# Polysketch attention with an MLP behind it: queries' features computed once and repeated through DRAM

## The chip, the cores and the metric

The kernel runs on one core of a Trainium2 chip. The metric is the device time of one execution in microseconds (us). The profile has a span of its own, a little shorter than that time, and all its positions are counted from the span's start. TensorE, VectorE, ScalarE and GpSimd are the four computing engines, each working through its instructions in the order of the program; SyncE issues nearly all transfers.

## What is computed

An attention block with features of degree two in place of the softmax, and an MLP block on its result, all in float32: batch 4, 4 heads, 1088 tokens, 32 values a head, so 128 for a token.

```python
def phi(x):                                   # S1, S2: 8 x 32
    a = np.einsum('rd,bhsd->bhsr', S1, x)     # 8 features
    b = np.einsum('rd,bhsd->bhsr', S2, x)     # 8 more
    return np.einsum('bhsi,bhsj->bhsij', a, b).reshape(*x.shape[:-1], 64)
q_p, k_p = phi(q), phi(k)
kv = np.einsum('bhsf,bhsd->bhfd', k_p, v)
z = np.sum(k_p, axis=2)
num = np.einsum('bhsf,bhfd->bhsd', q_p, kv)
den = np.einsum('bhsf,bhf->bhs', q_p, z)[..., None] + 1e-06
x = num / den                                 # heads side by side: 4 x 1088 x 128
xn = (x - mean(x)) / np.sqrt(var(x) + 1e-06) * g_ln
out = x + np.maximum(xn @ w_ch1, 0.0) @ w_ch2 # 128 -> 512 -> 128
```

The point for this change: a token and head have 16 features, 8 of S1 and 8 of S2, and the 64 values of phi are all products of one of the first with one of the second.

## The kernel before

**Chunks.** The tokens are worked on in nine chunks. Chunks 0 to 7 are halves of the four batch entries (chunk c is half c % 2 of entry c // 2), 512 tokens each, four tiles of 128. Chunk 8 (`LAST`) holds the 64 tokens that are left of each entry, 256 in all, two tiles.

**A chunk's stages.** `query_rows` (L376) turns the queries on VectorE in 32x32 blocks, so that the 128 partitions hold 4 heads x 32 values and the columns the tokens (`qT`). `query_features` (L389) makes the features with the partitions of the result standing for the 64 pairs (i, j), twice over for two halves of the tokens. It doesn't compute 16 features and repeat them: its weights `wa` and `wb` (32 x 64 for a head, L620) hold each row of S1 and of S2 eight times, so TensorE computes each of the 16 features eight times. These are 16 products of 32 rows by 64 columns, each over 256 columns of tokens (128 in chunk 8): for each of `wb` and `wa`, two halves and four heads, into PSUM banks 0 to 3. ScalarE copies the half of `wb` to SBUF (`qb`, L408), and VectorE multiplies it with that of `wa`, still in PSUM, into `qp` (L409), in two instructions each for two heads. `numerators` (L416) multiplies `qp` with the keys' sums `kvz` (L432, banks 0 and 1) and divides by the denominators (L439 to L447) to give `x`. `statistics` (L472 to L486) and `root` (L493 to L503) give mean and variance. `turn_x` (L514), or `send_x` with `blocks_x`, transposes x: from chunk 3 on, `send_x` (L518) writes x to DRAM in four transfers (L527), reads it back rearranged in one (`xb`, L533), and `blocks_x` (L540) turns it in blocks. `hidden` (L550, four times, with the ReLU on ScalarE at L553) and `second` (L563) are the MLP, `result` (L578) scales and adds, and four transfers write the output (L599).

The keys go the same way: `key_features` (L320, in PSUM, copied at L325), `key_products` (L338), `key_values` (L355, copied into `kvz` at L363 and L365). Theirs belong to batch entries 0 to 3, and are done by slot 4.

**Order.** There is no scheduler: each engine executes its instructions in the order in which the code emits them. That order is written out by hand, in a part ahead of the loop (to L733) and a loop over slots c = 2 to 8 (L735). Slot c computes the MLP of chunk c, the numerators of chunk c + 2, and, last, the query features of chunk c + 3 (L763):

```python
        if c < LAST:
            mlp_in(c, ...)          # hidden, 4 times
            root(c)
        numerators(c + 2)
        send_x(c + 2)
        ...
            second(c)
            query_rows(c + 3)
            result(c)
        query_features(c + 3)
```

SyncE too issues its transfers in this order, and waits in it: `xb` for the four writes of `rows`, the output for VectorE. Transfers take turns over eight completion semaphores, so that each can be issued only when the eighth ahead of it has landed.

**Buffers.** `qT`, `qb`, `qp`, `xb` and most other tiles of the pool `work` have two buffers; the DRAM tile `rows` and the output tile `ob` have three, `x` four.

Of the kernel before, what the change touches and what calls it, by code (L numbers as in the profile page):

```python
# [9 lines left out]
F32 = mybir.dt.float32  # L10
U32 = mybir.dt.uint32
AF = mybir.ActivationFunctionType
ALU = mybir.AluOpType
# [16 lines left out]
def kernel(  # L30
# [9 lines left out]
    moe_w_ch2: bass.AP,  # L40
    out: bass.AP,
):

# [17 lines left out]
    nc = tc.nc  # L63
# [24 lines left out]
    def bank(i):  # L88
        return banks[:, 512 * i : 512 * (i + 1)]
# [277 lines left out]
                kvp[F * (1 - i) : F * (2 - i), 0 : 2 * D1],  # L367
            )

    qTs, qps, xs, rs, mvs, xTs, hTs, xbs = {}, {}, {}, {}, {}, {}, {}, {}  # L370

    def query_steps(b):

# [15 lines left out]
    def query_features(c, between=None):  # L389
# [16 lines left out]
        for h in (2, 0):  # L406
# [6 lines left out]
            if h and between:  # L413
                between()

    def numerators(c):  # L416


        if c > LAST:
            return  # L420
        x = xs[c] = work.tile([P, 512], F32, tag="x", name="x", bufs=4)
        qp, n = qps.pop(c), ntiles(c) // 2
        step = 64 if c < LAST else 32
        for i in range(n):
            for h in range(H):
                for half in range(2):
                    rows = slice(F * half, F * half + F)
                    for u in range(0, P, step):
                        kvz = kvzs[CHUNKS[c][0] if c < LAST else u // 32]
                        t, o = 256 * h + P * i + u, W * i + D1 * h  # L430
                        z = D1 * (h // 2) + (0 if h % 2 == half else 2 * D1)
                        nc.tensor.matmul(  # L432
                            bank(half)[u : u + step, o : o + D1], qp[rows, t : t + step],
                            kvz[rows, z : z + D1], start=True, stop=True,
                        )
        den = small.tile([P, 4 * H], F32, tag="den", name="den")
        rden = small.tile([P, 4 * H], F32, tag="rden", name="rden")
        m = n * H
        nc.vector.tensor_scalar(  # L439
            out=_ap(den, 0, P, 0, [[m, 2], [1, m]]),  # L440
            in0=_ap(banks, 0, P, D, [[512, 2], [D1, m]]),
            scalar1=1e-6, scalar2=None, op0=ALU.add,
        )
        nc.vector.reciprocal(rden[:, 0 : 2 * m], den[:, 0 : 2 * m])
        for half in range(2):
            by_i, by_h = x_steps(c)
            nc.vector.tensor_tensor(  # L447
                out=_ap(x, 0, P, by_i * n * half, [[by_i, n], [by_h, H], [1, D]]),
                in0=_ap(banks, 0, P, 512 * half, [[W, n], [D1, H], [1, D]]),
                in1=_ap(rden, 0, P, m * half, [[H, n], [1, H], [0, D]]),  # L450
                op=ALU.mult,
            )
# [9 lines left out]
    def ntiles(c):  # L462
        return 4 if c < LAST else 2
# [54 lines left out]
    def send_x(c):  # L518

        if c > LAST:  # L520
            return
        x, m = xs[c], D * ntiles(c)
        xb = xbs[c] = work.tile([P, 512], F32, tag="xb", name="xb")

        rows = dram.tile([P, 4 * m], F32, tag="rows", name="rows", bufs=3)
        for p0 in range(4):
            nc.sync.dma_start(  # L527
                out=bass.AP(
                    rows.tensor, rows.offset + m * p0, [[4 * m, 32], [32 * 4 * m, H], [1, m]]
                ),  # L530
                in_=_ap(x, 32 * p0, 32, 0, [[m, H], [1, m]]),
            )
        nc.sync.dma_start(out=xb[:, 0 : 4 * m], in_=rows)  # L533
# [131 lines left out]
    w1_terms = w1_parts.terms(halves[1])  # L665
    fill(1)


    def keys(b, at):
        for part in range(3):  # L670
# [3 lines left out]
    def keys_in(b):  # L674
        for part in range(3):
            key_tokens(b, part, nc.gpsimd)
            key_rows(b, part)

    def mlp_in(c, between):

        for j in range(JC):
            if j in between:
                between[j]()
            hidden(c, j)
# [17 lines left out]
    for part in range(3):  # L702
# [8 lines left out]
    result(0)  # L711
    query_features(2)
    keys_in(2)

    mlp_in(1, {
        1: lambda: key_values(1, 7, 0, 4),
        2: lambda: query_features(3),
        3: lambda: key_values(1, 7, 4, NT),
    })
    root(1)  # L720
    numerators(2)
# [3 lines left out]
    query_rows(4)  # L725
    numerators(3)
    send_x(3)
    statistics(3)
    second(1, 2, 4)
    turn_x(2)  # L730
    result(1)
# [3 lines left out]
    for c in range(2, LAST + 1):  # L735

        b = (c + 3) // 2
        odd, some = c % 2 == 1, b < B
        if c == LAST - 1:
            blocks_x(LAST)  # L740
        if c < LAST:
            mlp_in(c, {2: lambda: key_values(b, 7, 5, NT)} if some and not odd else {})
            root(c)
        if c == LAST - 1:
            root(LAST)
        numerators(c + 2)
        send_x(c + 2)
        if some and odd:
            keys(b, (2, 3, 7))
        statistics(c + 2)  # L750
        if c < LAST - 1:
            blocks_x(c + 1)
        if c == LAST - 1:
            second(c, 0, 3)
            result(c, 0, 3)
            mlp_in(LAST, {})
            second(c, 3, 4)
            result(c, 3, 4)
        else:
            second(c)  # L760
            query_rows(c + 3)
            result(c)
        query_features(c + 3)  # L763
        if some and odd:
            key_values(b, 7, 0, 5)
        if b + 1 < B and not odd:
            keys_in(b + 1)
# [30 lines left out]
```

## Time and profile before

| | |
|---|---|
| time, median of 3 runs | 114.37 us (114.34 to 115.2) |
| span of the profiled execution | 112.6 us, 4412 instructions |
| TensorE, weight loads beside it | 103.8 us (92%), 73.3 us (65%) |
| VectorE | 62.1 us (55%) |
| ScalarE | 44.0 us (39%) |
| GpSimd | 41.4 us (37%) |
| transfers | 13.13 MB in 12835 packets, mean 117 GB/s |
| products of the query features: L400, `wb` and `wa` | 144 pieces each, 6.0 and 5.5 us busy |
| copies `qb` (L408), products `qp` (L409) | 18 each, 9.3 and 11.1 us busy |
| numerators (L432) | 576 pieces, 10.1 us busy |
| `hidden` (L550), `second` (L563) | 33.9 and 33.1 us busy |

How to read it: the profile calls TensorE's products PE and its weight loads PEld, VectorE DVE, ScalarE ACT, GpSimd POOL, and SyncE's issuing SPq. L400 is line 400 of the kernel. A float32 product appears as two pieces, so the 16 products of a chunk's query features are 32 pieces. Pieces overlap on the array, so their summed durations say less than the chain of work, which follows the end of the kernel back from each piece to what released it. TensorE's granted clock was 1.0 throughout.

### The profile page before, as it was taken

The page shows a single profiled execution, that of the slowest core. Times are in us where ns is not written, and L with a number is a line of the kernel's source. Part 1 is how long each engine was busy: PE and PEld are TensorE (multiplying, and loading weights), DVE is VectorE, ACT ScalarE, POOL GpSimd, SP SyncE. Part 2 cuts the span into 40 slices and gives each one's busy share as a digit, 9 for nine tenths or more (in the row PEclk, how much of TensorE's full clock was granted, in tenths as well). Part 3 has the DMA queues.
Part 4 walks back from the last instruction along what each step waited for, and adds up shares of the span by engine and source line. Part 5 has one row for each costly group of instructions (what it writes and reads, how often), then busy time and mean ns, then how long its engine had stood idle before and what let it go on. Part 6 is the DMA issues. An engine that isn't in the chain of part 4 may idle for free.

```text
span 112.6 us, 4412 instructions
## 1 busy us (share of the span) xinstructions
PE 103.8 (92%) x1875; PEld 73.3 (65%) x1875; DVE 62.1 (55%) x188; ACT 44.0 (39%) x104; POOL 41.4 (37%) x127
## 2 busy tenths in 40 slices
PE   6748889989999999999999999999999999999970
PEld 2336755489745799656953996579449739849760
DVE  1748974958985276621967746129618716320330
ACT  5126445660567430565036403640560262062500
POOL 4053037224898299501450596024003303205000
PEclk9999999999999999999999999999999999999999
DMA  0997999998992000461235043203340350240022
GB/s 12 271 196 218 325 262 243 291 159 266 275 263 89 9 9 0 99 163 29 51 67 167 6 93 124 71 0 74 66 145 13 87 189 6 47 135 4 0 70 70
DMA packets 12835, 13.13 MB, mean 117 GB/s; under 512 B 3472, under 2 KB 9872, under 8 KB 12816
## 3 DMA queue, kind: packets, MB, share of 16 engines
q1 hardware_dynamic: 12720, 12.79, 43.6%
q8 instruction: 14, 0.23, 0.9%
q10 hardware_dynamic: 96, 0.07, 0.3%
q14 instruction: 5, 0.04, 0.1%
HBM read 9.18 MB, written 3.67 MB: 114 GB/s over the span
## 4 chain that ended last, share of the span: by engine, by line
PE 81%; DMA 4%; DVE 4%; SPq 3%; ACT 2%; POOL 2%; issue 1%; ACTq 0%
PE banks L563 29%; PE banks L550 25%; PE banks L432 8%; PE banks L355 7%; PE banks L400 6%; DMA kn<-in_k_dram 4%; PE banks L320 3%; POOL w_cl L198 2%; SPq L126 2%; PE banks L514 1%; DVE qp L409 1%; PE banks L612 1%; SPq L114 1%; ACT xT L516 1%; DVE w_up L211 1%
## 5 line engine op out<-in xcount | busy, mean ns | idle before, releaser
L550 PE MATMUL banks<-xT,w 128*128 128x512 f32 (+1 forms) x72 | 33.9, 595 | 0.6 <-ACT xT L516 0.5
L563 PE MATMUL banks<-w,hT 128*128 128x128 f32 x272 | 33.1, 278 | 0.0
L563 PEld LDWEIGHTS banks<-w,hT 128*128 128x128 f32 x272 | 31.4, 192 | 1.1 <-DVE xT L540 0.2
L553 ACT ACTIVATE hT<-banks 128x512 f32<-128x512 f32 (+1 forms) x36 | 20.7, 574 | 17.5 <-PE banks L550 17.5
L550 PEld LDWEIGHTS banks<-xT,w 128*128 128x128 f32 x72 | 11.9, 189 | 13.3 <-ACT hT L553 5.8
L408 ACT COPY qb<-banks 128x512 f32<-128x512 f32 (+1 forms) x18 | 9.3, 564 | 22.3 <-PE banks L400 22.3
L338 POOL TENSOR_TENSOR kp<-fs 128x1024 f32<-128x1024 f32 (+2 forms) x11 | 15.4, 1426 | 4.8 <-ACT fs L325 4.6
L578 DVE SCALAR_TENSOR_TENSOR ob<-banks,rstd,x 128x128 f32<-128x128 f32 x34 | 9.8, 343 | 10.5 <-PE banks L563 3.7
L498 POOL TENSOR_TENSOR r<-va,r 128x4 f32<-128x4 f32 (+1 forms) x9 | 1.8, 199 | 36.5 <-DVE r L497 30.9
L409 DVE TENSOR_TENSOR qp<-banks,qb 128x512 f32<-128x512 f32 (+1 forms) x18 | 11.1, 656 | 4.6 <-ACT qb L408 4.6
L432 PEld LDWEIGHTS banks<-kvz,qp 64*64 64x64 f32 (+1 forms) x576 | 9.0, 131 | 6.5 <-ACT hT L553 1.5
L497 DVE RECIPROCAL r<-r 128x4 f32<-128x4 f32 (+1 forms) x9 | 1.5, 176 | 19.1 <-ACT r L493 19.1
L432 PE MATMUL banks<-kvz,qp 64*64 64x33 f32 (+1 forms) x576 | 10.1, 219 | 0.8 <-DVE qp L409 0.3
L355 PEld LDWEIGHTS banks<-v,kp 128*32 128x32 f32 (+3 forms) x504 | 7.0, 113 | 4.0 <-issue 1.5
L355 PE MATMUL banks<-v,kp 128*32 128x33 f32 (+3 forms) x504 | 7.9, 202 | 0.0
L400 PE MATMUL banks<-qT,wb 32*64 32x256 f32 (+1 forms) x144 | 6.0, 387 | 1.7 <-DVE qT L289 1.7
L472 DVE BATCH_NORM_STATS2 st<-x 128x6 f32<-128x128 f32 x34 | 7.3, 278 | 0.0
L447 DVE TENSOR_TENSOR x<-banks,rden 128x256 f32<-128x256 f32 (+1 forms) x18 | 6.5, 404 | 0.3
L289 DVE STREAM_TRANSPOSE qT<-qn 128x512 f32<-128x512 f32 x8 | 5.4, 686 | 1.5 <-DMA qn<-in_q_dram 1.5
L320 PE MATMUL banks<-sk,kT 128*64 128x64 f32 x136 | 5.4, 226 | 0.8 <-DVE kT L302 0.4
L320 PEld LDWEIGHTS banks<-sk,kT 128*64 128x64 f32 x136 | 4.7, 137 | 1.9 <-DVE kT L302 0.8
L400 PE MATMUL banks<-qT,wa 32*64 32x256 f32 (+1 forms) x144 | 5.5, 362 | 0.0
(70 smaller groups left out, 83.4 us busy)
## 6 DMA issues: line engine op xcount, KB each, us to landing
out_dram<-ob SPq DMA_DIRECT2D x33, 64.0 KB, 2.2
vn<-in_v_dram SPq DMA_DIRECT2D x16, 128.0 KB, 6.2
kn<-in_k_dram SPq DMA_DIRECT2D x3, 544.0 KB
qn<-in_q_dram SPq DMA_DIRECT2D x3, 544.0 KB
rows<-x SPq DMA_DIRECT2D x20, 64.0 KB, 1.8
xb<-rows SPq DMA_DIRECT2D x5, 256.0 KB, 2.8
kn<-in_k_dram SPq DMA_DIRECT2D x2, 256.0 KB, 3.2
w_raw<-in_moe_w_ch_dram SPq DMA_DIRECT2D x2, 256.0 KB, 2.9
```

The costliest lines, as they stand in the source:

```text
L320: nc.tensor.matmul(kf[u : u + 64, 64 * i : 64 * i + 64], kT[:, P * i + u : P * i + u + 64], sk, start=True, stop=True,)
L338: eng.tensor_tensor(out=_ap(kp, 0, m, (t0 + i0) * H * F, [[F, n], [R, R], [1, R]]), in0=_ap(kf, 0, m, o, [[R2, n], [1, R], [0, R]]), in1=_ ...
L355: nc.tensor.matmul(kvp[o : o + step, D1 * (h // 2) : D1 * (h // 2 + 1)], kp[0:m, H * F * t + f : H * F * t + f + step], v1[0:m, W * t + D1 ...
L400: nc.tensor.matmul(bank(h)[F * half : F * half + F, o : o + n], w[rows, :], qT[rows, n * half : n * half + n], start=True, stop=True,)
L408: nc.scalar.copy(own, _ap(banks, 0, P, 512 * h, [[512, 2], [1, n]]))
L409: nc.vector.tensor_tensor(out=_ap(p, 0, P, 256 * h, [[256, 2], [1, n]]), in0=_ap(banks, 0, P, 512 * h + 256, [[512, 2], [1, n]]), in1=own, ...
L432: nc.tensor.matmul(bank(half)[u : u + step, o : o + D1], qp[rows, t : t + step], kvz[rows, z : z + D1], start=True, stop=True,)
L472: nc.vector.bn_stats(out=st[:, 6 * i : 6 * i + 6], in_=x_tile(c, i))
L550: nc.tensor.matmul(hp[:, 0:n], w1[:, P * j : P * (j + 1)], xTs[c][:, 0:n], start=True, stop=True)
L553: nc.scalar.activation(hTs[c][:, 512 * j : 512 * j + n], hp[:, 0:n], AF.Relu)
L563: nc.tensor.matmul(second_at(c, i), hT[:, 512 * j + P * i : 512 * j + P * i + P], w2[:, DM * j : DM * (j + 1)], start=(j == 0), stop=(j == ...
L578: nc.vector.scalar_tensor_tensor(out=ob[:, t], in0=second_at(c, i), scalar=rstd[:, i : i + 1], in1=x_tile(c, i), op0=ALU.mult, op1=ALU.add,)
```

## The change

For chunks 5 to 8, TensorE computes each of the 16 features once. A new weight tile `wf` (128 x 40, built by GpSimd before the first slots) holds the 8 rows of S1 and of S2 by turns: columns 0 to 31 begin with S1's, columns 8 to 39 with S2's. `send_features` makes 16 products of 32 rows by 32 columns, over 128 columns of tokens (64 in chunk 8): for four quarters u of the tokens and four heads, into 32 partitions of bank h each. Of the 32 columns 16 are used, the two sets of features in one order for the first two quarters and in the other for the last two. One copy of 128 x 512 (ScalarE; VectorE for chunk 5) moves them to SBUF as `ff`, and four transfers write the 16 used partitions of each quarter to DRAM (`feat`, 2 KB a partition).

`spread_features` reads them back repeated: `qa` in one transfer in which each of 16 rows of 4 KB is repeated eight times in neighbouring partitions, and `qb` in two of 64 partitions, each of which repeats a group of eight rows eight times. `query_products` is then one multiplication of 128 x 1024, both operands in SBUF. Since tokens and heads lie in another order in `qp`, `numerators` reads other columns for these chunks.

The stages stand in other slots. The rows of chunk c + 5 are turned and its features made and sent at the end of slot c, where the features of chunk c + 3 were; chunk 6's are made in the middle of slot 2, ahead of the keys' values, and chunk 5's in the middle of slot 1, where VectorE copies them. The reads for chunk c + 4 follow `send_x` of chunk c + 2 in slot c, on the same queue of SyncE, behind those of x. The products of chunk c + 3 stand at the end of slot c. After slot 5 nothing is added. Chunks 0 to 4 keep the old way.

What it is for: TensorE does a smaller part of the array's work for these four chunks, since the repeating is left to the transfers.

```diff
--- before.py
+++ after.py
@@ -367,7 +368,7 @@
                 kvp[F * (1 - i) : F * (2 - i), 0 : 2 * D1],
             )
 
-    qTs, qps, xs, rs, mvs, xTs, hTs, xbs = {}, {}, {}, {}, {}, {}, {}, {}
+    qTs, frows, fqs, qps, xs, rs, mvs, xTs, hTs, xbs = {}, {}, {}, {}, {}, {}, {}, {}, {}, {}
 
     def query_steps(b):
 
@@ -413,6 +414,63 @@
             if h and between:
                 between()
 
+    def send_features(c, eng):
+
+
+
+
+        if c > LAST:
+            return
+        qT, w = qTs.pop(c), 32 * ntiles(c)
+        for u in range(4):
+            for h in range(H):
+                nc.tensor.matmul(
+                    bank(h)[32 * u : 32 * u + 32, 0:w],
+                    wf[D * h : D * h + D, R * (u < 2) : R * (u < 2) + 32],
+                    qT[D * h : D * h + D, w * u : w * u + w], start=True, stop=True,
+                )
+        ff = work.tile([P, 512], F32, tag="ff", name="ff")
+        o, i = _ap(ff, 0, P, 0, [[w, H], [1, w]]), _ap(banks, 0, P, 0, [[512, H], [1, w]])
+        if eng is nc.scalar:
+            eng.copy(o, i)
+        else:
+            eng.tensor_copy(out=o, in_=i)
+
+        rows = frows[c] = dram.tile([32, 8 * w], F32, tag="feat", name="feat", bufs=3)
+        for u in range(4):
+            nc.sync.dma_start(
+                out=bass.AP(
+                    rows.tensor, rows.offset + 8 * w * R2 * (u // 2) + 4 * w * (u % 2),
+                    [[8 * w, R2], [1, 4 * w]],
+                ),
+                in_=ff[32 * u : 32 * u + R2, 0 : 4 * w],
+            )
+
+    def spread_features(c):
+        if c not in frows:
+            return
+        rows, m = frows.pop(c), 256 * ntiles(c)
+        qa = work.tile([P, H * 256], F32, tag="qa", name="qa")
+        qb = work.tile([P, H * 256], F32, tag="qb", name="qb")
+        for t, r0, pat in (
+            (qa, R, [[m, R2], [0, R]]),
+            (qb[0:F], 0, [[0, R], [m, R]]),
+            (qb[F:P], 3 * R, [[0, R], [m, R]]),
+        ):
+            nc.sync.dma_start(
+                out=t[:, 0:m],
+                in_=bass.AP(rows.tensor, rows.offset + m * r0, pat + [[1, m]]),
+            )
+        fqs[c] = qa, qb
+
+    def query_products(c):
+        if c > LAST:
+            return
+        n = 256 * ntiles(c)
+        (qa, qb), p = fqs.pop(c), work.tile([P, H * 256], F32, tag="qp", name="qp")
+        qps[c] = p
+        nc.vector.tensor_tensor(out=p[:, 0:n], in0=qa[:, 0:n], in1=qb[:, 0:n], op=ALU.mult)
+
     def numerators(c):
 
 
@@ -420,7 +478,7 @@
             return
         x = xs[c] = work.tile([P, 512], F32, tag="x", name="x", bufs=4)
         qp, n = qps.pop(c), ntiles(c) // 2
-        step = 64 if c < LAST else 32
+        step, w = (64, 128) if c < LAST else (32, 64)
         for i in range(n):
             for h in range(H):
                 for half in range(2):
@@ -428,6 +486,8 @@
                     for u in range(0, P, step):
                         kvz = kvzs[CHUNKS[c][0] if c < LAST else u // 32]
                         t, o = 256 * h + P * i + u, W * i + D1 * h
+                        if c > 4:
+                            t = w * (H * ((P * i + u) // w) + h) + u % w
                         z = D1 * (h // 2) + (0 if h % 2 == half else 2 * D1)
                         nc.tensor.matmul(
                             bank(half)[u : u + step, o : o + D1], qp[rows, t : t + step],
@@ -664,6 +724,12 @@
     w2_parts.bound(full, nc.gpsimd)
     w1_terms = w1_parts.terms(halves[1])
     fill(1)
+
+    wf = consts.tile([P, 5 * R], F32, name="wf")
+    for w, o, step, n in ((wa, 0, R, 3), (wb, R, 1, 2)):
+        nc.gpsimd.tensor_copy(
+            out=_ap(wf, 0, P, o, [[R2, n], [1, R]]), in_=_ap(w, 0, P, 0, [[0, n], [step, R]])
+        )
 
 
     def keys(b, at):
@@ -711,11 +777,12 @@
     result(0)
     query_features(2)
     keys_in(2)
+    query_rows(5)
 
     mlp_in(1, {
         1: lambda: key_values(1, 7, 0, 4),
         2: lambda: query_features(3),
-        3: lambda: key_values(1, 7, 4, NT),
+        3: lambda: (key_values(1, 7, 4, NT), send_features(5, nc.vector)),
     })
     root(1)
     numerators(2)
@@ -725,7 +792,9 @@
     query_rows(4)
     numerators(3)
     send_x(3)
+    spread_features(5)
     statistics(3)
+    query_rows(6)
     second(1, 2, 4)
     turn_x(2)
     result(1)
@@ -736,15 +805,23 @@
 
         b = (c + 3) // 2
         odd, some = c % 2 == 1, b < B
+
+        def between():
+            if c == 2:
+                send_features(6, nc.scalar)
+            if some and not odd:
+                key_values(b, 7, 5, NT)
+
         if c == LAST - 1:
             blocks_x(LAST)
         if c < LAST:
-            mlp_in(c, {2: lambda: key_values(b, 7, 5, NT)} if some and not odd else {})
+            mlp_in(c, {2: between})
             root(c)
         if c == LAST - 1:
             root(LAST)
         numerators(c + 2)
         send_x(c + 2)
+        spread_features(c + 4)
         if some and odd:
             keys(b, (2, 3, 7))
         statistics(c + 2)
@@ -758,9 +835,10 @@
             result(c, 3, 4)
         else:
             second(c)
-            query_rows(c + 3)
+            query_rows(c + 5)
             result(c)
-        query_features(c + 3)
+        send_features(c + 5, nc.scalar)
+        query_products(c + 3)
         if some and odd:
             key_values(b, 7, 0, 5)
         if b + 1 < B and not odd:
```

## The prediction

> **What bounds the kernel now.** I read the page's busy shares first, then the chain of work that ended last in order of time, then the timeline of one slot, then the transfers by window. From the page:
>
> ```profile
> PE 103.8 (92%) x1875; PEld 73.3 (65%) x1875; DVE 62.1 (55%) x188; ACT 44.0 (39%) x104; POOL 41.4 (37%) x127
> ...
> PE   6748889989999999999999999999999999999970
> ...
> DMA  0997999998992000461235043203340350240022
> GB/s 12 271 196 218 325 262 243 291 159 266 275 263 89 9 9 0 99 163 29 51 67 167 6 93 124 71 0 74 66 145 13 87 189 6 47 135 4 0 70 70
> ```
>
> TensorE is busy in every slice from the ninth on (a slice is 2.8 us). The transfers are full for the first third, and mostly at 0 to 5 tenths after it. A busy share can hide waits, so the chain decides (start us, us, what):
>
> ```profile
> 45.37 1.05 PE banks L400 x32
> ...
> 51.99 1.07 PE banks L432 x64
> 53.06 3.77 PE banks L563 x32
> 56.83 1.05 PE banks L400 x32
> 57.88 3.79 PE banks L550 x8
> 61.66 1.07 PE banks L432 x64
> ...
> 67.69 1.05 PE banks L400 x32
> ...
> 79.05 1.05 PE banks L400 x32
> 80.10 3.79 PE banks L550 x8
> 83.89 1.07 PE banks L432 x64
> ...
> 88.72 0.62 PE banks L400 x32
> ...
> 93.13 0.69 PE banks L432 x47
> ```
>
> From 23 to 102 us the chain is TensorE alone, one piece ending where the next begins. So each microsecond taken off TensorE there comes off the end, until something else is late. The L400 pieces at 56.83, 67.69, 79.05 and 88.72 are the query features of chunks 5, 6, 7 and 8: 3 x 1.05 + 0.62 = 3.77 us. (The one at 45.37 is chunk 4, which stays as it is.)
>
> How late may the new work be? Slot 4 in the timeline:
>
> ```profile
> 79.14 1.12 DVE L578 SCALAR_TENSOR_TENSOR ob<-banks,rstd,x 128x128 f32<-128x128 f32 x4 [0.56 <-POOL va L486]
> 79.88 0.34 SPq L533 DMA_DIRECT2D xb<-rows  x1
> 80.21 1.07 ACT L408 COPY qb<-banks 128x512 f32<-128x512 f32 x2 [5.26 <-PE banks L400]
> 80.82 1.29 DVE L409 TENSOR_TENSOR qp<-banks,qb 128x512 f32<-128x512 f32 x2 [0.55 <-ACT qb L408]
> 83.82 1.14 PE L432 MATMUL banks<-kvz,qp 64*64 64x33 f32 x64
> ```
>
> The products qp are done at 82.11 and read at 83.82: 1.7 us of room, which the change alters but doesn't use up.
>
> [...] L550 streams 512 columns in 3.79 / 8 = 0.474 us, 0.93 ns a column; the 32 pieces of 256 columns of L400 would need 7.6 us one after another and took 1.05. Sixteen tiles no row here shows. [...] the trace has 0.69 us for L211 over 128x512, also two tensors. [...]
>
> **The change part by part.**
>
> TensorE, removed: 3.77 us. Added for each chunk: 16 products of 32 rows by 32 columns, which by the 32 pieces for 16 products at L400 are again 32 pieces, of 128 columns (64 for chunk 8). Upper bound: chunk 8's old form, also 128 columns a piece but on eight tiles, 0.62 us. Lower bound: two pieces of 128 columns on each of 16 tiles, 2 x 128 x 0.93 ns = 0.24 us[...]. Between them stands the rate at which small pieces with 32 weight columns are issued: L432 for chunk 8, 64 pieces in 0.69 us, 10.8 ns; L355 in the chain, 0.83 us for 80 pieces up to 0.92 for 64, so 10 to 14 ns. 32 x 12 ns = 0.38 us; I take it, and 0.35 for chunk 8. Added: 3 x 0.38 + 0.35 = 1.49. Net 3.77 - 1.49 = 2.28 us; bounds 1.4 (0.62 three times and 0.5) and 2.7.
>
> The new products' waits. Chunk 5's stand at 36.6 us and need banks 0 to 3 free of chunk 3's products; those end on VectorE at 36.60 (L409, 35.30 + 1.29). I count 0.1 us. Chunk 6's stand near 49.5 and need chunk 4's products, which end near 48.5, or 48.9 with the extra transpose ahead of them. No wait.
>
> VectorE. Two products (1.29 us) become one of 1024 columns[...]. It no longer waits for ScalarE, so in slot 4 it follows the last L578 and ends at about 2.4 us after the second products; they are read 3.8 us after them now that L400 is gone. Room 1.3 us: hidden. Chunk 5's transpose (0.69) moves to 34.12, where VectorE is idle for 1.18 us; its q landed by 29.4, for the queue held the next load of q until then. Chunk 6's goes ahead of the result at 45.04 and delays only that. The copy of chunk 5's features (about 0.65, by L409) lies in the 1.81 us idle ahead of L497 at 38.41.
>
> ScalarE loses two copies (1.07) and gets one (0.58); it is idle for 5.26 us ahead of them. GpSimd's two small copies for the weights lie in its 2.4 us idle before 21.82. Nothing for either.
>
> Transfers. Per chunk 128 KB are written and 1 MB is read (qa 512 KB, qb twice 256), half for chunk 8; 3.5 MB on top of 13.1. If qb runs on 8 engines, each of these carries 32 + 64 = 96 KB. The best window with long rows, 13 to 14 us, moved 378 GB/s (23.6 per engine), the page's slice at 11 us 325 (20), windows with the short rows of v near 200 (12.5). I take 20: 4.9 us, and 1.5 more to land (from L527, 64 KB in 1.8, and L533, 256 KB in 2.8). So 6.4 us after the issue. The reads of chunk 5 are issued near 47.9 and used near 58; those of chunk 7 near 70 and used near 79.6: hidden.
>
> But they add a wait: eight completion semaphores take turns, so the feature writes behind wait for these reads to land, and behind them on SyncE stand the next chunk's rows of x, then xb, then the next reads. That round takes 1.78 (rows) + 1.37 (they land) + 0.44 (xb) + 6.4 + 0.45 = 10.4 us. The two slots from 51.99 to 74.22 will take about 20.9. So the queue just keeps up at 20 GB/s an engine, and what it lags is taken from the room of xb and qb, some 3 to 4 us each. Cost: none.
>
> Sum: 114.37 - 2.28 + 0.1 = 112.2 us.
>
> **The rivals.** (1) The array doesn't pack sixteen tiles, and each chunk costs what chunk 8 did: 114.37 - 1.4 + 0.1 = 113.1. For it: no row shows sixteen. Against: four column groups (L355) and eight tiles pack well. (2) The reads are slower, 15 GB/s an engine: landing takes 8.1 us, the round 12.1. Followed on, rows of chunk 5 go out near 69 instead of 64, chunk 7's qb lands near 81.4 and holds L432 for 0.5 us, and xb of chunk 6 is 1.1 late: 112.2 + 1.6 = 113.8. For it: the repeats read the same few rows at once. Against: the long rows in the first third moved at 20 and more. (3) The reads run at 12.5: landing 9.4, the round 13.4; chunk 7's qb lands near 84.3, so L432 is 3.4 us late, and xb of 6 and qb of 8 add some 1.6: 112.2 + 5 = 117.2, slower than before. For it: windows of 200 GB/s in which the engines were full, and a queue with no slack. Against: those windows carried 1 KB pieces, these are 4 KB.
>
> **How the numbers follow.** Forecast 0.62, rival 1 0.10, rival 2 0.14, rival 3 0.14. The range takes in the lower bound of the added products (111.7, and a little) and rivals 1 and 2: 111.5 to 114.0. Faster by over 1% is below 113.2: forecast and rival 1, 0.72. Within 1%: rival 2, 0.14. Slower: rival 3, 0.14.
>
> **What would show it.** Right: four groups of new products of about 0.38 us in the chain, L400 gone after 46 us, and the chain still TensorE alone between 46 and 100 us. The packing is wrong if those groups take 0.6. The transfers are wrong if qa and qb take over 8 us to land, the products L472 wait for them, or the chain steps through qb or xb. If VectorE's copy at 37 us holds the numerators of chunk 2, the early transposes were mis-costed.

## The result, and the profile after

The changed kernel takes 121.39 us (median, 120.93 to 121.95), the kernel before beside it 114.78 us: a ratio of 1.056, with a 95% interval of 1.046 to 1.066. It is slower by 5.6%, and the time lies outside the range of 111.5 to 114.0. Some executions of a kernel come out up to a few per cent longer, mostly at a lower granted clock (the kernel before took 117.82 us at 0.956 and 114.05 at 0.998 on one chip), and the ratios here and below leave these out, so that a ratio need not be the quotient of two medians.

The profiled execution has a span of 119.2 us against 112.6. From the page: busy shares; TensorE, its granted clock and the transfers by slice (3 us); and the shares of the chain that ended last.

```profile
PE 104.3 (88%) x1875; PEld 74.1 (62%) x1875; DVE 62.2 (52%) x185; ACT 41.7 (35%) x99; POOL 42.0 (35%) x129
...
PE   6847889899999999999999999968449799999970
...
PEclk9999999999999999999999999999996899999999
DMA  1988999999930202296335953178531762514022
...
DMA 38%; PE 35%; SPq 11%; DVE 5%; ACT 3%; issue 3%; POOL 2%; ACTq 0%
```

TensorE was full to the end before. Now it has holes in the slices from 78 to 89 us, and in the two slices behind them, up to 95 us, its clock is lower. Nearly half of the chain is transfers and the queue that issues them. In order of time (start us, us, what), the chain leaves TensorE at 50.5 us, for good until 104:

```profile
49.88 0.59 PE banks L427 x32
...
50.50 0.59 ACT ff L435
...
51.18 7.68 DMA qb<-feat
...
58.87 0.30 SPq L441
...
60.65 1.78 DMA rows<-x
...
64.72 7.33 DMA qb<-feat
...
73.85 3.35 DMA rows<-x
...
79.04 7.79 DMA qb<-feat
...
88.63 3.20 DMA rows<-x
...
103.84 3.86 PE banks L610 x8
```

This is one queue, going round: the reads of qb land after 7.3 to 7.8 us; only then the feature writes (L441) go out that stand behind them (SyncE waits there for qb six times, 8.5 us in all), then the rows of x (L587), which land after 1.8 to 3.4 us, then xb and the next reads. What that does to the engines, from the timelines of VectorE and of TensorE (start, us, what, in brackets the idle time before it and what ended it):

```profile
80.07 0.71 DVE L600 STREAM_TRANSPOSE xT<-xb 128x512 f32<-128x512 f32 x1 [2.31 <-DMA xb<-rows]
86.85 1.23 DVE L472 TENSOR_TENSOR qp<-qa,qb 128x1024 f32<-128x1024 f32 x1 [5.07 <-DMA qb<-feat]
94.64 0.71 DVE L600 STREAM_TRANSPOSE xT<-xb 128x512 f32<-128x512 f32 x1 [3.27 <-DMA xb<-rows]
```

```profile
80.83 3.86 PE L610 MATMUL banks<-xT,w 128*128 128x512 f32 x8 [1.41 <-DVE xT L600]
88.13 1.14 PE L492 MATMUL banks<-kvz,qp 64*64 64x33 f32 x64 [3.44 <-DVE qp L472]
89.20 5.47 PE L623 MATMUL banks<-w,hT 128*128 128x128 f32 x32
95.41 3.00 PE L610 MATMUL banks<-xT,w 128*128 128x512 f32 x6 [0.74 <-DVE xT L600]
```

TensorE waits 1.41, 3.44 and 0.74 us (and 0.26 and 0.1 elsewhere), 6.0 us in all. The 32 pieces at 89.20 take 5.47 us instead of 3.84: the granted clock between 86 and 96 us was 0.83 on average. That is 1.6 us more. Against these stand the products saved: after 46 us, 3.77 - 0.43 - 0.43 - 0.56 = 2.4 us. (Chunk 8's group takes 0.56 us here. Where VectorE turns its queries in time, as in e1 and e3, it takes 0.32.) With the 0.7 us by which the changed kernel is behind at 45 us (0.51 of it chunk 5's new products) this gives 6.0 + 1.6 - 2.4 + 0.7 = 5.9 of the 6.6 us of span. The other 0.7 us lie in small gaps that were not followed.

These are TensorE's own books. The lower clock did not lengthen the kernel by itself: the chain doesn't pass through TensorE there, xb of chunk 6 landed at 94.6 us whatever TensorE did, and at full clock TensorE would, by an estimate from these numbers (0.74 + 1.6), have waited about 2.4 us for it instead of 0.74.

### The profile page after: what moved, and what is told of

The parts are those of the page before. It is cut to its first block, busy times and chain, and to the rows that moved or that the text cites. A ratio compares the mean times of both kernels' runs of the same rounds, so it can differ in the third digit from the quotient of the medians.

```text
span 119.2 us, 4448 instructions
## 1 busy us (share of the span) xinstructions
PE 104.3 (88%) x1875; PEld 74.1 (62%) x1875; DVE 62.2 (52%) x185; ACT 41.7 (35%) x99; POOL 42.0 (35%) x129
## 4 chain that ended last, share of the span: by engine, by line
DMA 38%; PE 35%; SPq 11%; DVE 5%; ACT 3%; issue 3%; POOL 2%; ACTq 0%
DMA qb<-feat 23%; PE banks L623 11%; DMA rows<-x 9%; PE banks L610 9%; DMA kn<-in_k_dram 4%; PE banks L492 4%; PE banks L356 3%; SPq L587 3%; SPq L460 3%; PE banks L401 3%; DMA xb<-rows 2%; PE banks L321 2%; DVE qp L410 2%; POOL w_cl L199 2%; SPq L127 1%
## 5 line engine op out<-in xcount | busy, mean ns | idle before, releaser
L610 PE MATMUL banks<-xT,w 128*128 128x512 f32 (+1 forms) x72 | 34.0, 596 | 2.8 <-DVE xT L600 2.1
L623 PE MATMUL banks<-w,hT 128*128 128x128 f32 x272 | 34.7, 287 | 0.0
L623 PEld LDWEIGHTS banks<-w,hT 128*128 128x128 f32 x272 | 33.0, 200 | 1.1 <-issue 0.5
L610 PEld LDWEIGHTS banks<-xT,w 128*128 128x128 f32 x72 | 11.9, 188 | 15.6 <-ACT hT L613 5.8
L600 DVE STREAM_TRANSPOSE xT<-xb 128x512 f32<-128x512 f32 (+1 forms) x6 | 4.0, 664 | 12.9 <-DMA xb<-rows 12.9
L472 DVE TENSOR_TENSOR qp<-qa,qb 128x1024 f32<-128x1024 f32 (+1 forms) x4 | 4.4, 1089 | 9.0 <-DMA qb<-feat 9.0
L356 PEld LDWEIGHTS banks<-v,kp 128*32 128x32 f32 (+3 forms) x504 | 6.9, 113 | 3.2 <-issue 1.0
L356 PE MATMUL banks<-v,kp 128*32 128x33 f32 (+3 forms) x504 | 7.8, 202 | 0.0
L410 DVE TENSOR_TENSOR qp<-banks,qb 128x512 f32<-128x512 f32 x10 | 6.5, 685 | 1.8 <-ACT qb L409 1.8
L507 DVE TENSOR_TENSOR x<-banks,rden 128x256 f32<-128x256 f32 (+1 forms) x18 | 6.5, 405 | 0.3
L409 ACT COPY qb<-banks 128x512 f32<-128x512 f32 x10 | 5.5, 587 | 2.4 <-PE banks L401 2.4
```

The lines of the kernel that those rows point to most:

```text
L356: nc.tensor.matmul(kvp[o : o + step, D1 * (h // 2) : D1 * (h // 2 + 1)], kp[0:m, H * F * t + f : H * F * t + f + step], v1[0:m, W * t + D1 ...
L409: nc.scalar.copy(own, _ap(banks, 0, P, 512 * h, [[512, 2], [1, n]]))
L410: nc.vector.tensor_tensor(out=_ap(p, 0, P, 256 * h, [[256, 2], [1, n]]), in0=_ap(banks, 0, P, 512 * h + 256, [[512, 2], [1, n]]), in1=own, ...
L507: nc.vector.tensor_tensor(out=_ap(x, 0, P, by_i * n * half, [[by_i, n], [by_h, H], [1, D]]), in0=_ap(banks, 0, P, 512 * half, [[W, n], [D1 ...
L610: nc.tensor.matmul(hp[:, 0:n], w1[:, P * j : P * (j + 1)], xTs[c][:, 0:n], start=True, stop=True)
L623: nc.tensor.matmul(second_at(c, i), hT[:, 512 * j + P * i : 512 * j + P * i + P], w2[:, DM * j : DM * (j + 1)], start=(j == 0), stop=(j == ...
```

## The experiments

A ratio is always to the kernel before on the same chip, with its 95% interval; where none is given, the runs scattered too much for one. In several profiles TensorE's granted clock was 0.5 for a stretch of 3 to 10 us, in which its pieces take up to twice as long (four pieces of L610 3.78 us instead of 1.98 in e1); where this bears on a time it is said.

### Which half costs: TensorE's part alone, the transfers alone

```diff
 # e3: chunks 6 to 8 neither write nor read
+        if c > 5:
+            return
         rows = frows[c] = dram.tile([32, 8 * w], ...)
 ...
-        (qa, qb), p = fqs.pop(c), work.tile(...)
+        (qa, qb), p = fqs[5], work.tile(...)
 # e4: the kernel before, with
+    ff = consts.tile([P, 512], F32, name="ff")      # a constant
+    def send_features(c): ...      # the four writes alone, from ff
+    def spread_features(c): ...    # the three reads, into qa and a tile qc that nobody reads
```

> The changed kernel without the transfers of chunks 6 to 8: their features are computed and copied, but neither written nor read, and their products take the tiles of chunk 5. TensorE's, ScalarE's and VectorE's work and its order are those of the changed kernel. The working of the prediction gives 112.2 us with all transfers hidden, 0.38 us for a chunk's new products. Theory (queue): 111.7 to 112.7 us. Rival (16 tiles don't pack): 113.1 us. Rival (VectorE's wider product or the earlier stages cost the time): above 114 us.

> The kernel before, with the changed kernel's transfers added in the same places of the queue: the four writes a chunk (of a constant tile instead of features) and the three reads, into tiles that nothing uses. Computing is that of before, and no product waits for a read. Theory (queue round): x's rows and xb come 1 to 10 us late, VectorE waits for xb, 117 to 120 us. Rival (only the products' wait for qb costs): 114.4 us, as before.

Measured: TensorE's part alone 113.58 us, ratio 0.987 (0.978 to 0.995). The transfers alone 124.57 us, ratio 1.079 (1.066 to 1.091). So the change's first half brings 1.2 us by the medians, 1.5 by the spans, and its second half costs nearly 10 without any product that waits for it. In the profile of the transfers alone only x is late: VectorE waits 7.5 us for xb. SyncE's timeline shows why (L424 the feature writes, L559 the rows of x):

```profile
66.61 0.34 SPq L565 DMA_DIRECT2D xb<-rows  x1
67.08 0.58 SPq L443 DMA_DIRECT2D qa<-feat  x1
67.71 1.23 SPq L443 DMA_DIRECT2D qc<-feat  x2
70.90 6.24 SPq L424 DMA_DIRECT2D feat<-ff  x4
77.24 1.81 SPq L559 DMA_DIRECT2D rows<-x  x4
```

The four feature writes, which take SyncE 0.31 us each in the changed kernel (L441, median), stand for 6.24 us behind the reads, and rows of x behind them. That the transfers cost more alone than in the changed kernel was not expected. TensorE's timeline shows where they bite harder:

```profile
98.58 0.73 PE L402 MATMUL banks<-qT,wb 32*64 32x128 f32 x16 [4.11 <-DVE qT L387]
```

Here, as in the kernel before, VectorE turns a chunk's queries just ahead of their features, and behind xT in its order. So when xb is late, TensorE waits for the queries too, 1.26 and 4.11 us. In the changed kernel both stand two slots earlier, when the queue lags less, and TensorE waits 0.26 us for the queries of chunk 8 alone. In this profile, of the longest of four executions (126.56 us), TensorE's clock was 0.5 from 96.6 to 103.4 us besides.

### What in the reads costs: bytes, engines, repeats

```diff
 # e7: half the columns of each read, used twice
-                out=t[:, 0:m],
+                out=t[:, 0 : m // 2],
-    ... pat + [[1, m]]
+    ... pat + [[1, m // 2]]
 # e2: qb in 16 groups of 4 rows instead of 8 of 8
-            (qb[0:F], 0, [[0, R], [m, R]]),
+            (qb[0:F], 0, [[0, R2], [m, R // 2]]),
 # e6: 128 different rows of q instead of 16 rows of feat, same shapes
 ...                              # other patterns: a stride for each row
-                in_=bass.AP(rows.tensor, rows.offset + m * r0, pat + [[1, m]]),
+                in_=bass.AP(q.tensor, q.offset + m * r0, pat + [[1, m]]),
 # e10: e6 and e2 together
```

> The changed kernel, but the reads bring only half of the columns of qa and qb, in the same number of transfers, and the products use them twice. This leaves out half of the reading. Theory (bytes in the round): the last read lands in 4 to 5 us, as chunk 8's did (4.2), the round shrinks from 13 to 15 us to 10 to 11.5, and the time is 113.5 to 116 us. Rival (the number of transfers and their issue sets the round): 119 us or more.

> The changed kernel, but each of the two qb transfers reads 4 rows repeated 16 times instead of 8 rows repeated 8 times: the same bytes, pieces and places, with a slowest dimension of 16 on the side of DRAM. This leaves out half of the pairs of features. Theory (eight engines carry qb, 96 KB each with qa's share, at some 12 GB/s): landing of the last read falls from 7.3 to 7.8 us to about 5, the round from 13 to 15 us to about 11, time 114 to 115.5 us. Rival (the repeated reading of the same rows sets the rate): landing stays above 7 us and the time at 119 us or more.

> The changed kernel, but qa and qb are read from q, as 128 different rows of 4 KB each, with the same number of transfers, bytes, pieces and slowest dimensions (16 for qa, 8 for qb). This leaves out the use of the features. Theory A (reading a few rows over and over makes the reads slow): the last read lands in about 5 us instead of 7.3 to 7.8, and the time falls to 115 to 118 us. Theory B (the eight engines of qb set it): no change of the landing, 120 us or more; the run with 16 engines gained 1.0 us of landing and 2 to 3 us of time.

> The changed kernel, but qa and qb are read from different rows of q, and those of qb with a slowest dimension of 16: both edits of the runs e2 and e6 together, bytes and number of transfers the same. This leaves out the use of the features. If eight engines and repeated rows are two separate causes of the slow reads, the last read lands in 4.5 to 5.5 us and the time is 115 to 117.5 us, under both single edits (119.0 and 118.4). If they are one cause, it stays at 118 to 119.5.

| | time, us | ratio | a read of qb lands after, chunks 5, 6, 7 |
|---|---|---|---|
| changed kernel | 121.39 | 1.056 (1.046 to 1.066) | 7.7, 7.3, 7.8 us (second read) |
| half the bytes (e7) | 113.88 | 0.990 (0.979 to 1.000) | not in the trace |
| qb in 16 groups (e2) | 119.01 | 1.036 (1.024 to 1.048) | 6.5, 6.7, 5.8 (second) |
| other rows (e6) | 118.38 (116.4 to 121.1) | none | 5.6, 4.6, 7.1 (first) |
| both (e10) | 118.12 (115.1 to 120.4) | none | 6.6, 5.7, 5.3 (first) |

Of a chunk's two reads of qb the trace shows the landing of one only, which is given; in e2, where both can be read, they differ by less than 0.2 us.

The same number of transfers at half the bytes takes all of the loss away. Starts of the rows of x in that kernel are 10.9, 11.9 and 7.9 us apart, against 13.2, 14.8 and 9.0 in the changed one:

```profile
57.23 1.83 SPq L590 DMA_DIRECT2D rows<-x  x4
...
68.12 1.83 SPq L590 DMA_DIRECT2D rows<-x  x4
...
80.04 1.83 SPq L590 DMA_DIRECT2D rows<-x  x4
...
87.92 2.29 SPq L590 DMA_DIRECT2D rows<-x  x4
```

The rows still go out 1.6, 3.4, 2.9 and 2.4 us after their x is complete, but this lag doesn't grow, and TensorE waits for neither xb nor qb before 96 us. So it is bytes, not the number of transfers or their issue. The number of groups and the repeated rows each hold part of it, 0.6 to 2.7 us of a landing, and both together gain no more in sum than the repeats alone. The times of e2 and e10 missed what had been expected (114 to 115.5 and 115 to 117.5). Those of e6 and e10, which read other data, scatter by 5 us, so how groups and repeats share the rest stays open.

### The place on the queue, and another queue

```diff
 # e1: the reads at the slot's end, behind the feature writes (SyncE)
         send_x(c + 2)
-        spread_features(c + 4)
 ...
         send_features(c + 5, nc.scalar)
+        spread_features(c + 4)
 # e5: reads issued by GpSimd, place as in the changed kernel; e8: by ScalarE
-            nc.sync.dma_start(
+            nc.gpsimd.dma_start(        # e8: nc.scalar
 # e9: e1's place and GpSimd's queue
```

> The changed kernel with one edit: the reads qa and qb are issued at the end of a slot, behind the output and the feature writes, instead of behind xb. Bytes, engines and work are the same. Theory (the round on SyncE's queue: each feature write waits for the completion semaphore of the reads eight transfers ahead, and the rows of x stand behind it): from slot 2 on only output transfers then wait for the reads, xb comes in time, and what is left is the reads of chunk 7, issued some 5 us later in the slot, about 1 us late: 113 to 114.5 us. Rival (the volume: 1 MB a chunk slows x's own transfers, whatever the order): no gain, 119 us or more. Rival (TensorE's side doesn't gain): not under 115 us.

> The changed kernel with the three reads of a chunk issued by GpSimd instead of SyncE, at the same place of the program: another queue, with semaphores of its own, on the same 16 engines. Bytes the same. Theory (what stands behind the reads on SyncE's queue waits for their data, by the semaphores in the changed kernel, by the queue's own order in the run with the reads last): rows of x land in about 2 to 3 us, xb is in time, 112.5 to 115 us. Rival (the engines' throughput is short, whatever the queue): 118 us or more. Rival (GpSimd's own time to make up a transfer delays the keys' products): a TensorE wait for kp in slot 3, 114 to 117 us.

> The changed kernel with the three reads of a chunk issued by ScalarE instead of SyncE, at the same place of the program, so on ScalarE's queue; about 1.8 us of issuing per slot on an engine that is busy 35% of the time. Theory (the order on SyncE's queue): as for GpSimd's queue, 112.5 to 115 us. Rival (throughput): 118 us or more. Rival (ScalarE's issuing delays the ReLUs): waits of TensorE for hT of 1 us a slot, 114 to 117 us.

> The changed kernel with the reads issued by GpSimd, and at the end of the slot, behind the keys' products and the feature writes, so that GpSimd doesn't stand waiting for feature writes ahead of the keys' products. Two runs suggest it: with the reads last on SyncE's queue the rows right behind them took 7 us to land, and with the reads on GpSimd's queue ahead of the products those came 4.3 us late. Theory (only what is ordered behind the reads suffers): neither holds here, the last read lands in 7 to 9 us with more than a slot of room, 112.5 to 114.5 us, faster than before. Rival (the engines' throughput, shared by the queues, is what delays x's transfers): xb takes 5 us or more to land and comes late, 116 us or more.

None of the four reached the time of the kernel before, though the theory had put all of them at 112.5 to 115 us. At the slot's end (e1): 125.57 us, ratio 1.092 (1.083 to 1.101). No wait for a semaphore of the reads stood ahead of the rows of x any more, yet SyncE's timeline shows xb 8.6 us behind rows that went out right after the reads:

```profile
67.03 0.57 SPq L460 DMA_DIRECT2D qa<-feat  x1
67.64 1.22 SPq L460 DMA_DIRECT2D qb<-feat  x2
68.96 1.82 SPq L587 DMA_DIRECT2D rows<-x  x4
77.57 0.34 SPq L593 DMA_DIRECT2D xb<-rows  x1
```

The rows took up to 7.6 us to land, a size that mostly takes 1.8 us before. So these small transfers were late behind large reads on their queue without a semaphore of the reads ahead of them; what held them up there, the traces don't show. TensorE never waits for that xb. What the late rows hold up is all that stands behind them on the queue, the next reads too, which go out at 82.35 us:

```profile
76.73 0.32 PE L356 MATMUL banks<-v,kp 64*32 64x33 f32 x4 [4.11 <-issue]
...
92.19 1.93 PE L492 MATMUL banks<-kvz,qp 64*64 64x33 f32 x64 [2.51 <-DVE qp L472]
```

The chain runs through rows, xb and these reads to the wait for qp, and then through TensorE at a clock of 0.5 until 98.9 us. The stop of 4.11 us ahead of it, in which TensorE waits for nothing that the profile shows, comes back below.

By GpSimd, 124.63 us, ratio 1.077 (1.053 to 1.100), for another reason: GpSimd had to wait for the feature writes to land, and the keys' products stood behind its reads. From the timelines of GpSimd and TensorE:

```profile
72.54 0.62 POOL L460 DMA_DIRECT2D qa<-feat  x1 [5.80 <-DMA feat<-ff]
73.16 1.12 POOL L460 DMA_DIRECT2D qb<-feat  x2
74.27 4.46 POOL L339 TENSOR_TENSOR kp<-fs 128x1024 f32<-128x1024 f32 x3
```

```profile
76.31 1.11 PE L356 MATMUL banks<-v,kp 128*32 128x33 f32 x64 [4.30 <-POOL kp L339]
```

Even there an xb landed only 7.5 us after its issue, from another queue. The two queues share the 16 DMA engines: in e9, below, the packets of the queue that carries SyncE's transfers took 50.5, 62.5 and 56.3% of the engines' time in the three microseconds from 54 us on, those of GpSimd's reads 47.3, 45.6 and 43.8%. By ScalarE, 122.64 us, ratio 1.065 (1.046 to 1.084): ScalarE stood 8.2 us ahead of the keys' copy L326 and 6.5 us ahead of the features' copy L435, and the keys were late.

GpSimd at the slot's end, 119.47 us, ratio 1.023 (1.014 to 1.031), has no wait for xb or qb on TensorE's path at all: once an xb took 8.8 us to land, as the rival had it, but it was not late. Instead TensorE stopped, with nothing that it waited for. From the chain of the execution that was profiled, the longest of six (121.76 us):

```profile
54.29 1.05 PE banks L492 x58
55.34 4.42 issue
59.76 0.43 PE banks L492 x4
```

The stop comes after 58 of the 64 pieces, and the 32 pieces of L623 behind it take 6.57 us instead of 3.77, at a clock of 0.5. At the same piece there is a shorter stop in five other kernels with chunk 5's reads. The trace of the transfers has a queue that it calls instruction, with 14 packets and 0.23 MB, so 16 KB each. That it brings TensorE's instructions is not shown; it is inferred from what follows. Where its packet starts (us), and where TensorE goes on:

| kernel | packet | TensorE goes on |
|---|---|---|
| reads last (e1) | 51.9 | 54.23, after a stop of 0.47 |
| TensorE's part alone (e3) | 52.0 | 54.42, after 0.49 |
| reads by GpSimd (e5) | 53.0 | 55.46, after 1.14 |
| other rows (e6) | 51.7 | 54.34, after 1.05 |
| half the bytes (e7) | 51.4 | 53.99, after 0.89 |
| GpSimd at the slot's end (e9) | 57.3 | 59.76, after 4.42 |
| changed kernel | 51.5 | no stop |
| reads last (e1), the stop at L356 | 74.0 | 76.73, after 4.11 |

TensorE goes on 2.3 to 2.7 us after the packet's start each time. In e9 the packets of GpSimd's queue fill the 16 DMA engines to 101% and 92% of their time from 51 to 53 us, and output transfers issued then took 8.5 us to land. That the reads made the packet late is argued from these times.

### Does the lag add up?

If one round of the queue takes 13 to 15 us and a slot 9 to 12.5, fewer or more widely spaced chunks should cost nothing.

```diff
 # e11: chunks 6 and 8 alone, reads on SyncE, place as in the changed kernel
-    spread_features(5)
-                        if c > 4:
+                        if c in (6, 8):
 ...                              # 5 and 7: query_rows, query_features as before
 # e12: chunks 6, 7, 8, from e9: GpSimd, at the slot's end
-    spread_features(5)
-                        if c > 4:
+                        if c > 5:
             if c == 2:
                 send_features(6, nc.scalar)
+            elif c == 3:
+                send_features(7, nc.scalar)
 ...                              # 5: query_rows, query_features as before
 # e13: e12 with the reads on SyncE, behind those of x
-            nc.gpsimd.dma_start(
+            nc.sync.dma_start(
         send_x(c + 2)
+        spread_features(c + 4)
```

> Only chunks 6 and 8 go the new way, with their transfers where the changed kernel has them (SyncE, behind those of x, in slots 2 and 4); chunks 5 and 7 are made the old way, so slot 3 brings no reads. TensorE saves 0.62 us for chunk 6 and 0.29 for chunk 8, by the pieces measured: 0.9 us. Theory: a round on SyncE with reads takes 13 to 15 us and one without about 8, the lag of one new round is 2 to 4 us, which is what xb and qb have of room, and it is made up in the slot without reads. So nothing on TensorE waits and the time is about 0.9 us below that of the kernel before: 113.3 to 114.2, ratio 0.988 to 0.997. Rival: each chunk's reads cost by themselves what four cost together divided by three and a half (8 to 10 us with TensorE's part, so 2.3 to 2.8 us a chunk, 1.2 to 1.4 for chunk 8), whatever lies between: 114.4 + 3.8 - 0.9, about 117.

> Chunks 6, 7 and 8 go the new way, chunk 5 the old; the reads are issued by GpSimd at the end of a slot, behind the feature writes, chunk 7's features are made in the middle of slot 3. So no read is in flight when the numerators of chunk 4 run near 56 us, where the version with all four chunks showed TensorE stopped for 4.4 us with nothing to wait for. TensorE saves 2 x 0.62 + 0.29 = 1.5 us. Theory A (that stop is caused by reads in flight): it is gone at that place, no xb or qb is late, and the time is 112.9 to 113.9, ratio 0.982 to 0.993; should a stop of the kind come with the first reads again, it stands elsewhere. Theory B (the stop belongs to that place of the program): 1 us or more again inside the numerators of chunk 4, and 114 to 118.

> Chunks 6, 7 and 8 go the new way and chunk 5 the old, as in the version before this one, but the reads are issued where the changed kernel has them: on SyncE, right behind the transfers of x. Against the changed kernel that leaves out chunk 5's reads alone (and moves chunk 7's features to the middle of slot 3). Theory (the lag of the queue of SyncE adds up from slot to slot, by 13 to 15 us a round against slots of 9 to 12.5): one full round fewer, so the rows of x of chunk 5 go out near 66 us instead of 72.5, those of chunk 6 near 80 instead of 87, and xb of chunk 6 lands near 85, ahead of the first MLP product of its chunk at 89. Nothing on TensorE waits by more than 0.5 us: 112.9 to 114, ratio 0.982 to 0.995. Rival (a queue shared with the transfers of x is what costs, and it was GpSimd's queue that repaired it): TensorE waits for xb or qp in slots 5 and 6 as in the changed kernel, 115.5 to 118.

Measured: chunks 6 and 8 alone, 113.40 us, ratio 0.982 (0.975 to 0.989). Three chunks by GpSimd, 113.34 us, ratio 0.983 (0.975 to 0.991). Three chunks on SyncE, 117.96 us (115.8 to 118.3), against 114.30 before. The first two are faster than both kernels, and can't be told apart. How large the gain is stays less sure than these intervals say: the kernel before took 113.69 to 116.50 us on that chip, and against its four shortest times, 114.3 on average, it is 1.1 and 0.9%.

How far the queue lags can be read from two rows for each chunk: the end of its x on VectorE (L507, L447 before) and the first issue of its rows (L587, L527), in us:

| | chunk 4 | 5 | 6 | 7 |
|---|---|---|---|---|
| before | 0.0 | 0.0 | 0.0 | 0.0 |
| changed kernel | 3.8 | 7.9 | 10.3 | 5.6 |
| 6, 7, 8 on SyncE (e13) | 0.0 | 2.5 | 5.4 | 5.5 |
| 6 and 8 on SyncE (e11) | 0.0 | 0.0 | 0.0 | 0.0 |
| 6, 7, 8 by GpSimd (e12) | 0.0 | 1.7 | 0.0 | 0.0 |

For example, chunk 6 of the three chunks on SyncE (VectorE, SyncE and TensorE's timelines):

```profile
77.91 0.76 DVE L507 TENSOR_TENSOR x<-banks,rden 128x256 f32<-128x256 f32 x2
...
91.43 0.71 DVE L600 STREAM_TRANSPOSE xT<-xb 128x512 f32<-128x512 f32 x1 [3.22 <-DMA xb<-rows]
```

```profile
84.03 1.83 SPq L587 DMA_DIRECT2D rows<-x  x4
...
88.65 0.34 SPq L593 DMA_DIRECT2D xb<-rows  x1
```

```profile
92.19 3.86 PE L610 MATMUL banks<-xT,w 128*128 128x512 f32 x8 [2.31 <-DVE xT L600]
```

x is complete at 78.67 and its rows go out at 84.03, 5.4 us later. In the changed kernel and in e13, each slot with a full chunk's reads on SyncE adds 2.4 to 4.1 us of lag. That is the theory. In e11 it had led me to expect 2 to 4 us of lag after chunk 6's reads, made up in the slot without reads; none arose. SyncE's timeline shows why:

```profile
63.77 0.64 SPq L460 DMA_DIRECT2D qa<-feat  x1
64.46 1.27 SPq L460 DMA_DIRECT2D qb<-feat  x2
65.77 2.33 SPq L659 DMA_DIRECT2D out_dram<-ob  x4
69.06 2.97 SPq L587 DMA_DIRECT2D rows<-x  x4
```

Chunk 7 goes the old way there, so no feature writes stand between these reads and the next rows to wait for the reads. So e11 takes away two things at once, and no run shows lag being made up in a slot without reads.

In e13 the theory's size was wrong: I had put the rows of chunk 6 at 80 us, by rounds of 13.5 us; the second round took 15.2 us (rows 68.86 to 84.03), and TensorE waited 2.3 us instead of at most 0.5. So the time was the rival's, with a lag of 5.4 us after two full rounds. The bytes are the same in e12 and e13, so bytes alone don't cost the time; but the queue and the place of the reads in the slot both change between them, and which of the two counts is not shown.

In e12 TensorE's longest wait from 44 to 100 us is 0.21 us, and the stop at piece 59 is gone:

```profile
52.75 1.14 PE L492 MATMUL banks<-kvz,qp 64*64 64x33 f32 x64
```

No reads are in flight there now, and the instruction packet started at 51.4 us instead of 57.3. That fits, but it isn't a clean test: chunk 5's 32 new pieces no longer stand ahead of this place, so that a late packet need not stop TensorE at piece 59 here.

## Why the prediction was wrong

**TensorE's part was right in the main.** The chain and the timelines have 0.51, 0.43, 0.43 and (in e1 and e3) 0.32 us for the four groups of new products (0.38 three times and 0.35 predicted), 1.69 instead of 1.49 in sum. The 32 pieces of 32x32 take 0.43 us where chunk 8's 32 pieces of 32x64, also over 128 columns, took 0.62, so rival 1 falls. One after another, at the 0.93 ns a column of L550, they would need 3.8 us; that all sixteen tiles of the prediction's lower bound (0.24 us) work at once is not shown. Chunk 5's start at 36.77 where 36.6 had been put. The part alone gave -1.2 us in the medians and -1.5 in the span, where -2.2 had been predicted, so it came out above the 111.7 to 112.7 us expected of it; 0.49 of the 0.7 us by which the span misses is the stop at piece 59, and 0.2 the new products.

**VectorE's part was right.** L472 takes 1.22 us, where the two products that it replaces took 1.29. (L211, read beforehand as an example, works on the bits of whole numbers and is no product.) Nothing on ScalarE or GpSimd stood in the way.

**The step that failed is the round of SyncE's queue: "So the queue just keeps up at 20 GB/s an engine ... Cost: none."** The mechanism was named there; its terms were too small. The round from 59.27 to 72.47, term by term:

| term | predicted | measured |
|---|---|---|
| rows issued and landed | 1.78 + 1.37 | 3.16 |
| xb, to the first read | 0.44 | 1.03 |
| first read to the issue of the last | not counted | 1.22 |
| the last read lands | 6.4 | 7.38 |
| a feature write, then rows | 0.45 | 0.41 |
| sum | 10.4 | 13.2 |

Of the 2.8 us, 2.2 lie between the first read's issue and the last landing, 8.6 us instead of 6.4: 1.2 pass while the reads are still being issued, which was put at nothing, and 1.0 is the landing. The other 0.6 is xb. In the next round rows landed 3.35 us after the last issue instead of 1.78, and it took 14.8. Against a slot of 10.4 us, itself the mean of a long and a short one (12.6 and 9.7 us before), the queue had no slack at all, so every term that grew was lag, and it grew from slot to slot.

**Rival 3 had the story**, with a round of 13.4 us. It put TensorE's wait for chunk 7's qp at 3.4 us, and it was 3.44; that is in part chance, since qb landed 2.5 us later than it said (86.8 instead of 84.3) and TensorE came late to it as well. It got 0.14, because the rate of 12.5 GB/s was held against windows of 1 KB pieces. In the changed kernel 1 MB takes 8.6 us from the first issue to the last landing (63.46 to 72.06), 122 GB/s for the core. Counted as the prediction counts, 96 KB an engine in 8.6 - 1.5 us, that is about 14 GB/s an engine, an estimate, between rivals 2 and 3. The repeats, which were named for rival 2, are part of that, the number of groups another; neither is most of it. The 96 KB rest on the prediction's assumption that qb runs on 8 of the 16 engines; the trace fits it, since all 16 together were busy 95 to 99% of the time in each microsecond from 64 to 68 us, and 55 to 60% from 69 to 72, when qa had landed (69.2).

**What rival 3 lacked.** It had the kernel 2.8 us behind the kernel before, and the span is 6.6 behind. Of the 3.8 us between, 1.4 are the wait for xb of chunk 5, which it didn't name. Some 0.9 more were lost behind the wait for qp, 2.5 instead of 1.6, with the 1.6 us at the lower clock counted as time in which xb was awaited. 0.5 are missing in TensorE's gain, 0.3 is a wait for turned queries, and the rest is the small gaps.

The clock: a granted clock of 0.5 followed the wait of 3.44 us, but also waits of 2.51 us (e1) and 1.39 us (e2), and none followed waits of 2.27 us (e6) and 2.31 us (e13). So the length of a single wait doesn't settle it, and why the clock fell stays open.

**What was to show it** did: L472 waited for qb, and the chain went through qb. A read of qb took 7.3 to 7.8 us to land, and the three reads together 8.6.

## What to carry to other kernels

Before a transfer is put on a queue that other work passes through, add up that queue's whole round, with every issue and every landing, and set it against the shortest slot. Here a round that by the prediction's 10.4 us just kept up took 13.2 and 14.8 us, and the lag grew by 2.4 to 4.1 us in each slot with a full chunk's reads on SyncE. Spacing the chunks, or moving the reads to a queue with nothing urgent behind it, at a point where their input has landed, kept part of the gain: two chunks of the four, or three by GpSimd, were 1 to 2% faster than the kernel before, where all four were 5.6% slower.

## What the runs showed of the hardware

- Small transfers behind large reads on one queue took about as long as these (7.3 to 7.8 us for a read of qb in the changed kernel): the rows of x, 64 KB, mostly 1.8 us before and up to 7.6 us right behind 1 MB (e1). On another queue it was not always better: xb, 256 KB, 2.7 to 3.2 us before, took up to 7.5, 8.8 and 7.9 us where GpSimd issued the reads (e5, e9, e12).
- The trace lists 14 packets of a queue called instruction among those of the 16 DMA engines. In e9, after reads that filled these to 101 and 92% from 51 to 53 us, one came 5.8 us later than in the changed kernel (57.3 instead of 51.5 us), and TensorE stopped for 4.4 us, which the profile shows as "issue". In seven stops TensorE went on 2.3 to 2.7 us after such a packet's start.
- Thirty-two pieces of 32x32 over 128 columns took 0.43 us in the chain, 13 ns a piece, and over 64 columns 0.32 us (e1, e3), 10 ns: half the columns saved a quarter of the time.
